# The first loads of a gated attention kernel: x's first piece in two transfers, the last two pieces merged, fifteen products of ones instead of seventeen

## The chip, the cores and the metric

The kernel runs on one core of a Trainium2 chip. Its time is the device time of one execution in microseconds (us). Several executions are timed and the median is given; one more execution is recorded by the hardware profiler, and its own time is given beside them. The core has engines that work side by side, each with its own list of instructions: TensorE (PE, whose weight loads are listed apart as PEld), VectorE (DVE), ScalarE (ACT), GpSimd (POOL) and SyncE (SP), which here only issues transfers (DMA). Engines wait for one another through semaphores.

## The reference

The input x has 2048 rows of 512 numbers. Three things are computed from it and mixed.

```
g = sigmoid((x * gate_w).sum(-1, keepdims=True))
qkv = x @ wqkv                       # 32 heads of width 16
scores = q k^T * 16**-0.5            # keys 0 to 255 places back, else -1e9
a = (softmax(scores) @ v) @ wo
b = (sigmoid(x @ w_gate) * (x @ w_up)) @ w_down      # inner width 1376
out = g * a + (1 - g) * b
```

All inputs are 32-bit floats. The change touches only the beginning of the product that gives v, x times the value weights (the last 512 columns of `wqkv`, called `wv` in the kernel).

## The kernel before, in words

Every large product is taken in three parts so that its precision holds: each 32-bit operand is split into a high part, which is a rounded copy in the format that TensorE multiplies, and a low part, the operand less its high part. Then high times high, high times low and low times high are summed in PSUM. The high part is made by a copy (mostly on ACT, in places on DVE), the low part by a subtraction on DVE, which therefore needs the high part first.

x comes transposed, as `xT`, in four chunks of 512 rows; each chunk consists of four pieces d = 0 to 3 of 128 input columns (the partitions) by 512 rows (the free dimension, called columns of a piece below). The value weights `wv` also have four pieces d of 128 by 512. Piece d of x and piece d of `wv` belong together: v for a block of 128 rows is the sum over the four d of three products each. One piece of either is 256 KB. They land in parts of one large buffer, which the profile calls `V` (`xraw` and `wvraw` in the code). High parts go to `xh` and `w` (`wvh` in the code), low parts to `xl` and `wvl`.

The program starts like this. PE multiplies ones by ones 17 times (L222, output `warm_ps`, 256 columns each), whose result nobody reads. SP issues the transfers of the pieces in the order wv0, x0, wv1, x1, wv2, x2, wv3, x3 (L230, L231), then two transfers of query and key weights (L180) and those of the next chunks of x (L206). ACT copies each piece of `wv` to its high part (L232) and, for pieces 0 and 1, the last 256 columns of x (L239); for pieces 2 and 3 it copies all of x. DVE copies the first 256 columns of x for piece 0, in two copies of 128 columns (L238), and for piece 1 in one, and makes all the low parts (L227). An engine takes its instructions in this written order.

PE then makes v of the first four blocks (L566, 48 products, output `vps`): for d = 0 and d = 1 in order high-high, high x with low weights, low x with high weights for the first two blocks and then again for the other two; for d = 2 each of the three kinds for all four blocks; for d = 3 block by block. In every product a block of x (128 by 128) is the operand that is loaded (PEld) and the weights (512 columns) stream past it. So `xh` of a block must be there before the load of its product begins. After that come the first projections (L300), and the long main part, in which attention, projections and the gated unit are interleaved by a written order on PE, ACT, DVE and SP (the scheduler is manual for these four; POOL is not touched here).

The order on SP matters too: the transfers share eight semaphores in turn, so that the ninth waits until the first has landed, and so on.

Of the kernel before, what the change touches and what calls it, by code (L numbers as in the profile page):

```python
# [14 lines left out]
P = 128  # L15
# [3 lines left out]
ND = D // P  # L19
# [4 lines left out]
CH = 512  # L24
# [46 lines left out]
def gated_mix_kernel(  # L71
# [11 lines left out]
    nc = tc.nc  # L83
# [68 lines left out]
    with ExitStack() as actx:  # L152
        apool = actx.enter_context(tc.tile_pool(name="apool", bufs=1))
        xh = apool.tile([P, ND, T], F32R, name="xh")
# [42 lines left out]
        xraw = Vf[:, NB * VROW + 16 - 2 * ND * CH:NB * VROW + 16].rearrange("p (c d t) -> p c d t", c=2, d=ND)  # L197
        wvraw = Vf[:, 0:ND * D].rearrange("p (d n) -> p d n", d=ND)
# [3 lines left out]
        wv_v = wv.rearrange("(c p) n -> p c n", p=P)  # L202
# [17 lines left out]
        def idle_mm(n):  # L220
            for _ in range(n):
                mm(warm_ps[:, 0:2 * P], ones[:, 0:P], ones[:, 0:2 * P], start=True, stop=True)  # L222

        idle_mm(17)

        def lower(lo, src, hi):
            nc.vector.tensor_tensor(lo, src, hi.bitcast(F32), op=ALU.subtract)  # L227

        for d in range(ND):
            nc.sync.dma_start(wvraw[:, d], wv_v[:, d])  # L230
            nc.sync.dma_start(xraw[:, 0, d], xT[0, d])  # L231
            nc.scalar.copy(wvh[:, d], wvraw[:, d])  # L232
            parts = ((0, 1), (1, 2), (2, 4)) if d == 0 else ((0, 2), (2, 4)) if d == 1 else ((0, 4),)
            parts = [slice(a * P, b * P) for a, b in parts]
            if d:
                lower(wvl[:, d], wvraw[:, d], wvh[:, d])
            for ts in parts[:-1]:
                nc.vector.tensor_copy(xh[:, d, ts], xraw[:, 0, d, ts])  # L238
            nc.scalar.copy(xh[:, d, parts[-1]], xraw[:, 0, d, parts[-1]])  # L239
            if d == 0:  # L240
                lower(wvl[:, d], wvraw[:, d], wvh[:, d])
            for ts in [slice(h * CH // 2, (h + 1) * CH // 2) for h in range(2)] if d < 2 else parts:
                lower(xl[:, d, ts], xraw[:, 0, d, ts], xh[:, d, ts])
# [48 lines left out]
        parts = {}  # L292
# [847 lines left out]
        for n, (c, f) in enumerate(steps):  # L1140
# [42 lines left out]
            for t in range(4):  # L1183
                ts = slice(t * P, (t + 1) * P)
# [79 lines left out]
```

## Time and profile before

| | |
|---|---|
| median of 3 runs | 706.84 us (706.81 to 707.37) |
| profiled execution | 706.25 us, of which the span from its first to its last instruction is 704.5 us |
| PE busy in the span | 700.3 us (99%) |
| DVE, ACT, POOL busy | 502.4 us, 436.0 us, 174.1 us |
| DMA | 127.40 MB, mean 181 GB/s |

In the rows of the timeline, the first number is the start in us from the span's beginning, the second how long the row lasts; a row can merge several instructions of one kind that follow each other (x2, x17). A bracket at the end of a row tells how long the engine had been idle before it, and what ended that. A row of SPq is the issue of a transfer, not the transfer itself.

### The profile page before, as it was taken

How to read it: one execution, taken by the hardware profiler on the slowest of the kernel's cores; microseconds unless marked ns; L12 is line 12 of the kernel's file. 1: busy time of each engine (PE TensorE's matmuls, PEld its weight loads, DVE VectorE, ACT ScalarE, POOL GpSimd, SP SyncE). 2: the span in 40 equal slices, each digit the busy share in tenths (PEclk: the TensorE clock that was granted, in tenths of full speed). 3: DMA queues.
4: the chain of work that ended last, by engine and by line, in shares of the span. 5: the costliest groups of instructions: out<-in, count | busy, mean ns of one | idle time of the engine just before them, and what ended most of it. 6: DMA issues, size and time to landing. Idle time of an engine off the chain costs nothing.

```text
span 704.5 us, 20403 instructions
## 1 busy us (share of the span) xinstructions
PE 700.3 (99%) x7721; PEld 613.2 (87%) x7721; DVE 502.4 (71%) x1488; ACT 436.0 (62%) x889; POOL 174.1 (25%) x254
## 2 busy tenths in 40 slices
PE   9999999999999999999999999999999999999998
PEld 7888888999888889999888888899998888888886
DVE  5368877777777776777777777786667868567481
ACT  6422777677677677767767767765685745435241
POOL 5200333233243233323324323332360000000000
PEclk9999999999999999999999999999999999999999
DMA  8466735746455364572755628564676879778521
GB/s 306 120 182 209 221 126 182 208 132 217 143 183 180 130 227 158 171 229 68 231 168 187 215 71 268 160 220 123 205 199 218 258 195 246 178 185 238 148 65 60
DMA packets 102685, 127.40 MB, mean 181 GB/s; under 512 B 45666, under 2 KB 62306, under 8 KB 102588
## 3 DMA queue, kind: packets, MB, share of 16 engines
q1 hardware_dynamic: 102444, 125.97, 58.7%
q8 instruction: 61, 1.00, 0.6%
q14 instruction: 36, 0.29, 0.1%
q10 hardware_dynamic: 144, 0.13, 0.1%
HBM read 71.80 MB, written 51.13 MB: 174 GB/s over the span
## 4 chain that ended last, share of the span: by engine, by line
PE 99%; DVE 0%; issue 0%
PE gu L300 29%; PE pj L300 12%; PE st L452 6%; PE s L390 6%; PE tp L667 6%; PE pd L101 5%; PE pd L99 5%; PE pd L100 5%; PE pv_st L488 5%; PE vh L704 4%; PE pv_s L488 3%; PE pv L488 2%; PE pa L99 2%; PE pa L100 2%; PE pa L101 2%; PE vps L566 2%
## 5 line engine op out<-in xcount | busy, mean ns | idle before, releaser
L396 DVE CUSTOM_DVE_ANT_0 junk<-s,mask 128x384 f32<-128x384 f32 (+2 forms) x512 | 272.0, 531 | 103.2 <-PE s L390 38.8
L300 PE MATMUL gu<-xh,w 64*128 64x512 f32 x1152 | 270.1, 391 | 0.0
L458 ACT ACTIVATE pbuf<-st 128x384 f32<-128x384 f32 x320 | 155.4, 495 | 53.3 <-PE st L452 24.3
L300 PE MATMUL gu<-xl,w 64*128 64x512 f32 x576 | 182.3, 389 | 0.0
L452 PE MATMUL st<-ring 64*128 64x384 f32 (+2 forms) x536 | 165.8, 322 | 0.0
L390 PE MATMUL s<-ring 64*128 64x384 f32 (+2 forms) x536 | 162.3, 321 | 0.0
L300 PEld LDWEIGHTS gu<-xh,w 64*128 64x128 f32 x1152 | 151.4, 184 | 10.0
L464 POOL TENSOR_SCALAR_AFFINE_SELECT pbuf<-pbuf 128x512 f32<-128x512 f32 x80 | 56.0, 700 | 260.6 <-ACT pbuf L458 245.2
L390 PEld LDWEIGHTS s<-ring 64*128 64x128 f32 x536 | 94.8, 184 | 11.8 <-DVE mx L396 1.2
L452 PEld LDWEIGHTS st<-ring 64*128 64x128 f32 x536 | 97.8, 184 | 7.6 <-issue 1.4
L458 ACT ACTIVATE V<-st 128x384 f32<-128x384 f32 (+2 forms) x192 | 81.9, 440 | 32.5 <-PE s L390 18.1
L300 PEld LDWEIGHTS gu<-xl,w 64*128 64x128 f32 x576 | 88.5, 184 | 2.7
L300 PE MATMUL pj<-xl,wqh 64*128 64x512 f32 (+1 forms) x228 | 79.2, 388 | 0.0
L300 PE MATMUL pj<-xh,wqh 64*128 64x512 f32 (+1 forms) x228 | 79.2, 389 | 0.0
L300 PE MATMUL pj<-xh,wql 64*128 64x512 f32 (+1 forms) x228 | 69.6, 388 | 0.0
L100 PE MATMUL pd<-ring,hb 128*128 128x512 f32 x160 | 62.3, 389 | 0.0
L101 PE MATMUL pd<-ring,hb 128*128 128x512 f32 x160 | 62.3, 389 | 0.0
L99 PE MATMUL pd<-ring,hb 128*128 128x512 f32 x160 | 62.3, 389 | 0.0
L95 ACT CAST hb<-V 128x512 fp32r<-128x512 f32 x40 | 24.9, 622 | 55.5 <-DVE V L876 47.5
L470 POOL TENSOR_SCALAR_AFFINE_SELECT pbuf<-pbuf 128x512 f32<-128x512 f32 x80 | 53.8, 673 | 0.0
L464 POOL TENSOR_SCALAR_AFFINE_SELECT V<-V 128x512 f32<-128x512 f32 x48 | 31.8, 663 | 76.4 <-ACT V L458 53.0
L627 ACT COPY sp<-gu 128x512 f32<-128x512 f32 x72 | 42.2, 586 | 9.8 <-PE gu L300 7.8
(157 smaller groups left out, 1387.2 us busy)
## 6 DMA issues: line engine op xcount, KB each, us to landing
gu_scratch<-sp SPq DMA_DIRECT2D x72, 256.0 KB
V<-gu_scratch SPq DMA_DIRECT2D x34, 512.0 KB
ring<-stack_scratch SPq DMA_DIRECT2D x56, 256.0 KB
stack_scratch<-sh SPq DMA_DIRECT2D x14, 512.0 KB
stack_scratch<-sl SPq DMA_DIRECT2D x14, 512.0 KB
ring<-stack_scratch SPq DMA_DIRECT2D x14, 512.0 KB
guraw<-in_wgu_dram SPq DMA_DIRECT2D x18, 256.0 KB
v_scratch<-V SPq DMA_DIRECT2D x4, 1088.0 KB
```

The costliest lines, as they stand in the source:

```text
L99: mm(ps, lh, rh, start=first, stop=False)
L100: mm(ps, lh, rl, start=False, stop=False)
L101: mm(ps, ll, rh, start=False, stop=last)
L300: return mm(pt, (wl if w == 2 else wh)[r, d], (xl if w == 1 else xh)[r, d, c * CH:(c + 1) * CH], start=k == 0 and not second, stop=k == 3 ...
L390: mm(pt[:, (k - k0) * P:(e - k0) * P], lhsT, blk(g, k, hh, 1, e - k), start=k == k0, stop=e == i + 1, skip_group_check=True,)
L396: nc.vector.tensor_tensor_reduce(junk[:, 0:n], pt[:, 0:n], mask[:, 3 * P - n:], scale=1.0, scalar=NEG, op0=ALU.add, op1=ALU.max, accum_out ...
L452: mm(pt[:, (q - j) * P:(e - j) * P], lhsT, blk(g, q, hh, 0, e - q), start=q == j, stop=e == last, skip_group_check=True,)
L458: exps.append(nc.scalar.activation(buf[:, s0:s0 + 2 * n, hh], pt[:, 0:n * P].rearrange("p (k t) -> p k t", t=HB), AF.Exp, scale=SCALE,))
L464: nc.gpsimd.affine_select(buf[:, s0:s0 + 2], buf[:, s0:s0 + 2], pattern=[[HB, 2], [0, HG], [1, HB]], compare_op=ALU.is_ge, fill=0.0, base= ...
L470: nc.gpsimd.affine_select(old, old, pattern=[[-HB, 2], [0, HG], [-1, HB]], compare_op=ALU.is_gt, fill=0.0, base=0, channel_multiplier=1,)
L488: mm(bank[32 * hh:32 * hh + w, o + k * HB:o + e * HB], vt[HB * half:HB * half + HB, v:v + w], p_run(g * NB + j, hh, half, k, e), start=fir ...
L667: return mm(tp[b][:, 0:TW], (xl if w == 1 else xh)[r, d, b * P:(b + 1) * P], tw[d][int(w == 2)][r, 0:TW], start=k == 0 and not second, sto ...
```

## The change

The first transfer of x is cut into two: its first 128 columns (rows of 512 bytes), then the other 384. The pieces 2 and 3 of `wv` come in one transfer of 512 KB, and then pieces 2 and 3 of x in one. The transfers are now issued in the order wv0, x0 columns 0 to 127, x0 columns 128 to 511, wv1, x1, wv2 with wv3, x2 with x3: seven instead of eight. Of piece 0 the copy of columns 128 to 255 goes from DVE to ACT. Two products of ones are left out. Everything else stands as it did, so that the lines from there on have numbers higher by four.

```
-        idle_mm(17)
+        idle_mm(15)
...
         for d in range(ND):
-            nc.sync.dma_start(wvraw[:, d], wv_v[:, d])
-            nc.sync.dma_start(xraw[:, 0, d], xT[0, d])
+            if d < 3:
+                ds = slice(d, d + 1 if d < 2 else ND)
+                nc.sync.dma_start(wvraw[:, ds], wv_v[:, ds])
+                for ts in (slice(0, P), slice(P, CH)) if d == 0 else (slice(0, CH),):
+                    nc.sync.dma_start(xraw[:, 0, ds, ts], xT[0, ds, :, ts].rearrange("d p t -> p d t"))
             nc.scalar.copy(wvh[:, d], wvraw[:, d])
             parts = ((0, 1), (1, 2), (2, 4)) if d == 0 else ((0, 2), (2, 4)) if d == 1 else ((0, 4),)
             parts = [slice(a * P, b * P) for a, b in parts]
             if d:
                 lower(wvl[:, d], wvraw[:, d], wvh[:, d])
-            for ts in parts[:-1]:
+            for ts in parts[:1] if len(parts) > 1 else []:
                 nc.vector.tensor_copy(xh[:, d, ts], xraw[:, 0, d, ts])
-            nc.scalar.copy(xh[:, d, parts[-1]], xraw[:, 0, d, parts[-1]])
+            for ts in parts[min(1, len(parts) - 1):]:
+                nc.scalar.copy(xh[:, d, ts], xraw[:, 0, d, ts])
```

On SP the list begins like this before (`in_wv_dram` and `in_xT_dram` are the two inputs, `V` the buffer):

```order
L230 DMA V<-in_wv_dram 128x512
L231 DMA V<-in_xT_dram 128x512
L230 DMA V<-in_wv_dram 128x512
L231 DMA V<-in_xT_dram 128x512
L230 DMA V<-in_wv_dram 128x512
L231 DMA V<-in_xT_dram 128x512
L230 DMA V<-in_wv_dram 128x512
L231 DMA V<-in_xT_dram 128x512
```

and like this with the change:

```order
L232 DMA V<-in_wv_dram 128x512
L234 DMA V<-in_xT_dram 128x128
L234 DMA V<-in_xT_dram 128x384
L232 DMA V<-in_wv_dram 128x512
L234 DMA V<-in_xT_dram 128x512
L232 DMA V<-in_wv_dram 128x2x512
L234 DMA V<-in_xT_dram 128x2x512
```

The second piece of the weights moves from third to fourth place, and x2 can no longer land ahead of x3, nor wv2 ahead of wv3.

On ACT, after the load of its table, the list before is, up to the first weights of a projection (`w` is the high part of `wv`):

```order
L232 CAST w_70<-V 128x512
L239 CAST xh<-V 128x256
L232 CAST w_70<-V 128x512
L239 CAST xh<-V 128x256
L232 CAST w_70<-V 128x512
L239 CAST xh<-V 128x512
L232 CAST w_70<-V 128x512
L239 CAST xh<-V 128x512
L189 CAST wqh_142<-wqraw_130 128x512
```

and with the change:

```order
L235 CAST w_70<-V 128x512
L243 CAST xh<-V 128x128
L243 CAST xh<-V 128x256
L235 CAST w_70<-V 128x512
L243 CAST xh<-V 128x256
L235 CAST w_70<-V 128x512
L243 CAST xh<-V 128x512
L235 CAST w_70<-V 128x512
L243 CAST xh<-V 128x512
L189 CAST wqh_139<-wqraw_127 128x512
```

One copy of 128 columns is added between the first weights and the last half of x0; the order of the copies of pieces 2 and 3 is unchanged.

## The prediction

> **What bounds the kernel now.** First the page: how busy the engines are, and of what the chain that ended last is made.
>
> ```profile
> span 704.5 us, 20403 instructions
> PE 700.3 (99%) x7721; PEld 613.2 (87%) x7721; DVE 502.4 (71%) x1488; ACT 436.0 (62%) x889; POOL 174.1 (25%) x254
> PE 99%; DVE 0%; issue 0%
> ```
>
> PE sets the end. A change at the start is worth as much as it moves PE's first useful products, as long as nothing later lets PE wait. So I read the chain in order of time over its first 30 us:
>
> ```profile
> 0.84 3.78 PE warm_ps L222 x17
> 4.62 11.43 PE vps L566 x48
> 16.05 8.16 PE pj L300 x36
> ```
>
> The 36 products behind take 8.16/36 = 0.227 us each. At that pace the 48 products of L566 would need 10.88 us; they take 11.43. So slow clock and waits cost this stage 0.55 us, and what stands before it is the products of ones. **This bounds the whole prize to well under 1 us**, against some 1.4 us (0.2%), which is about what a measurement of this kernel tells from no change. Next the timeline, where PE begins:
>
> ```profile
> 3.52 0.62 ACT L232 CAST w<-V 128x512 fp32r<-128x512 f32 x1 [1.44 <-DMA V<-in_wv_dram]
> 4.12 0.36 DVE L238 CAST xh<-V 128x128 fp32r<-128x128 f32 x2 [4.12 <-DMA V<-in_xT_dram]
> 4.40 0.69 DVE L227 TENSOR_TENSOR wvl<-V,w 128x512 fp32r<-128x512 f32 x1
> 4.47 0.51 PEld L566 LDWEIGHTS vps<-w,xh 128*128 128x128 f32 x2 [0.33 <-ACT w L232]
> 4.50 1.12 PE L566 MATMUL vps<-w,xh 128*128 128x512 f32 x2
> 5.06 0.56 PE L566 MATMUL vps<-w,xh 128*128 128x512 f32 x1
> 5.45 0.62 PE L566 MATMUL vps<-wvl,xh 128*128 128x512 f32 x2
> L222 PE MATMUL warm_ps<-const-bfloat16-1.0 128*128 128x256 bf16 x17 | 3.8, 414 | 0.8 <-PEq L1251 0.8
> ```
>
> Of the 3.78 us of ones, 0.41 is the length of the last record, so 16 steps take 3.37 us: 0.21 us per product of 256 columns, or 0.42 for 512, nearly twice the 0.227 of later. PE runs at half pace here. The second and third useful products start 0.39 apart (5.06, 5.45), between the two paces, so the pace changes inside the second one, by this at about 5.4 us. The ones run out at 0.84 + 17 x 0.213 = 4.47, and just then the first load starts, although weights (3.52 + 0.62 = 4.14) and the first 128 columns of x (half of 0.36 after 4.12, about 4.35) are there. **The ones end the first wait**, by about 0.1 us.
>
> **The head, part by part.** Two ones less free PE at 0.84 + 15 x 0.213 = 4.04. Then the weights are last, at 4.14, if the 128 columns land sooner than the whole piece did (4.12). A quarter of the bytes, behind the same wv0, lies between wv0's landing (3.52) and 4.12; I take 3.7, and DVE's copy ends before 4.0. The first load then starts at 4.16 instead of 4.47. Its stream begins where the second load can follow; before, the second product's start less one slow pitch (5.06 - 0.42) gives 4.64, 0.17 behind the load, so now 4.33. At the slow pace products two and three start at 4.75 and 5.17; if the pace still changes at 5.4, the third does 0.23/0.42 of its work before and ends at 5.4 + 0.45 x 0.227 = 5.50. Before, the fourth started one fast pitch after 5.45, at 5.68. The head gains **0.18 us**. The second block's columns are now copied by ACT behind the weights, after the transfer of 384 columns: with that landed by 4.2 and 0.2 us for the copy they are there at 4.45, in time for 4.75. Bounds: nothing, if the 128 columns land no sooner than 4.12; 0.3 us, if the slow pace were no cost.
>
> **Piece 1 takes the gain away.** These are the rows of its chain:
>
> ```profile
> 1.72 0.43 SPq L230 DMA_DIRECT2D V<-in_wv_dram  x1
> 2.19 0.43 SPq L231 DMA_DIRECT2D V<-in_xT_dram  x1
> 5.95 0.62 ACT L232 CAST w<-V 128x512 fp32r<-128x512 f32 x1 [1.43 <-DMA V<-in_wv_dram]
> 6.61 0.69 DVE L227 TENSOR_TENSOR wvl<-V,w 128x512 fp32r<-128x512 f32 x1 [0.85 <-ACT w L232]
> 7.21 0.29 DVE L238 CAST xh<-V 128x256 fp32r<-128x256 f32 x1
> 7.62 0.30 PEld L566 LDWEIGHTS vps<-w,xh 128*128 128x128 f32 x2 [0.15 <-issue]
> 7.72 0.62 PE L566 MATMUL vps<-w,xh 128*128 128x512 f32 x2
> 4.10:5.90 1.80, 1.80 (x7) 1.21 (x6) 1.64 (x5) 0.43 (x2) 0.00 (x0) 1.00 0.96 239
> ```
>
> wv1 lands at 5.95; ACT copies it, DVE makes its low part and only then copies x1's first 256 columns, done at 7.50. PE's load idled for them until 7.62, and the product came at 7.72: from 5.45 that is ten products in 2.27 us, 0.227 each. So PE lost nothing here, but with nothing to spare: a normal load runs 0.22 us ahead of its product (10.22 and 10.45 below), this one only 0.10. The change leaves this chain as it is. So an earlier PE waits here, and the 0.18 is lost unless wv1 lands sooner. It is issued one place later, at 2.19 instead of 1.72 (the rows' step of 0.47). That is no delay in itself: it was under way for 4.2 us, with the DMA engines 0.96 busy in the last row (4.10 to 5.90), so it waits for the engines and not for its issue. What is ahead of it are the same bytes in one more transfer. Bounds: 0.2 sooner (as much as PE could use) to 0.47 later; I take **0.0**, nearest to the row of busy engines.
>
> **Pieces 2 and 3.** Here the merged transfers decide:
>
> ```profile
> 7.87 0.62 ACT L232 CAST w<-V 128x512 fp32r<-128x512 f32 x1 [0.86 <-DMA V<-in_wv_dram]
> 8.51 0.62 ACT L239 CAST xh<-V 128x512 fp32r<-128x512 f32 x1
> 9.20 0.62 ACT L232 CAST w<-V 128x512 fp32r<-128x512 f32 x1
> 9.82 0.62 ACT L239 CAST xh<-V 128x512 fp32r<-128x512 f32 x1
> 9.86 0.33 SPq L206 DMA_DIRECT2D V<-in_xT_dram  x1
> 10.22 0.87 PEld L566 LDWEIGHTS vps<-w,xh 128*128 128x128 f32 x4
> 10.45 1.07 PE L566 MATMUL vps<-w,xh 128*128 128x512 f32 x4
> 9.50:10.00 0.50, 0.50 (x4) 0.38 (x4) 0.50 (x2) 0.50 (x2) 0.00 (x0) 1.00 1.12 410
> ```
>
> Before, x2 was copied from 8.51 and x3 from 9.82. PE wants x2's high part when piece 2 begins (load 10.22, product 10.45) and had it at 9.13, 1.1 us early. Merged, x2 counts as landed with x3. x3 had landed by 9.82 (SP's next transfer, which waits for the same semaphore, goes out at 9.86). The bytes ahead are the same, so I let the pair land at 9.82: ACT copies x2 until 10.44. From the end of such a copy to the product it took 7.72 - 7.50 = 0.22 in piece 1, so piece 2 begins at 10.66 instead of 10.45: **0.21 us lost**. Bounds: the last row shows 410 GB/s and full engines, where 256 KB take 0.64 us; if the pair is done half a piece sooner (0.32), nothing is lost, and with wv1 early some 0.2 is even kept; a whole piece later (0.64) makes it 0.85 lost. I take the middle, as the bytes are equal and one fixed end goes with each merger.
>
> [...]
>
> **What else moves, and what covers it.** Behind 10.45 ACT runs later by about 1.2 us, since x2's copy, the weights' second copy and x3's copy all stand behind 9.82: 10.44, 11.06, 11.68 instead of 10.44 for the last. The work behind it:
>
> ```profile
> 10.48 1.27 ACT L189 CAST wqh<-wqraw 128x512 fp32r<-128x512 f32 x2
> 13.16 0.39 PE L566 MATMUL vps<-w,xh 128*128 128x512 f32 x1
> 14.11 0.59 ACT L570 COPY V<-vps 128x512 f32<-128x512 f32 x1 [1.08 <-PE vps L566]
> 15.88 0.39 PE L300 MATMUL pj<-xh,wqh 128*128 128x512 f32 x1
> 10.65 0.58 POOL L267 MEMSET V<- 128x256 f32 x1 [6.96 <-DMA V<-in_xT_dram]
> 18.80 0.59 ACT L324 CAST sh<-pj 128x512 fp32r<-128x512 f32 x1 [1.61 <-PE pj L300]
> ```
>
> Piece 3 is wanted at 13.16 and there at 11.7, its low parts by 12.4. The projection weights (ACT L189) end near 13.0 instead of 11.75, wanted at 15.88. The 1.08 us that ACT idled before L570 take up most of the delay, the 1.61 before L324 the rest. POOL's memset waits for the last low part of the weights and goes from 10.65 to about 11.9; L570 needs it at 14.1. If these covers failed, each would cost at most what it is late, 0.1 to 0.2 us. The added copy on ACT (about 0.2 us) ends before wv1 lands at 5.95; the shorter DVE list brings its first subtraction 0.2 us forward. One transfer less on SP (0.43) lies beside full DMA engines.
>
> **Sum.** The waits follow each other and the last decides: 0.18 gained at the head, taken back at piece 1, and 0.21 lost at piece 2. The profiled execution, 706.25 with its span of 704.5 and 1.75 around it, would become 706.46. The runs' median is 0.59 above it; on it the same 0.21 gives **707.05 us**.
>
> **Rivals.** First, **the gain is kept**: wv1 lands 0.2 sooner and the merged x by 9.4, as less is issued. For it: the merged pairs save two ends of transfers; against it: full engines. Time 706.84 - 0.18 = 706.66, at most 706.5.
>
> Second, **the change doesn't do what it says**: the first 128 columns land with the whole piece, near 4.1. Then the first load is at about 4.37, little is gained, and the later waits decide as before: 707.05 as well, so it counts with the forecast.
>
> Third, on the other side, **the slow pace goes on**. The pace changed at 5.4, that is 4.6 us after PE began at 0.84. With two ones less PE stands idle from 4.04 to about 4.3, and longer in an execution in which wv0 lands late. If what releases the pace needs unbroken work, the count begins anew at 4.3 and ends at 8.9: 3.5 us more at half pace, in which 3.5 x (1 - 0.227/0.42) = 1.6 us of work is lost. It decides as soon as the gap is longer than the switch bears; before, it bore the 0.17 us between the last of the ones (4.47) and the first stream (4.64). Time 707.05 + 1.6 = 708.65. The granted clock (third number from the end) reads 1.00 in the row of 4.10 to 5.90 too, so it doesn't show the slow stage; the products' steps do.
>
> [...]
>
> Fourth, **the merged x lands far later**, because one late DMA engine now holds up 512 KB. For it: wv1 landed 5.95 - 4.12 = 1.83 us behind x0, where a piece takes 0.64 at the full rate, so something held it up by 1.2 us. Against it: pieces 2 and 3 followed each other in 0.6 to 0.7 us before (8.51, 9.20, 9.82). Such a hold-up in the merged x costs 1.2 us: 708.25.
>
> **Chances.** Forecast with the second rival 0.71; gain kept 0.19; slow pace 0.06; late x 0.03; something later in the program that a shift by 0.2 us sets off, with either sign, 0.01. Faster by over 0.2% would need 1.4 us where 0.55 are to be had: 0.01. Slower by over 0.2%: 0.07. Within: 0.92. The forecast's bounds are 706.6 (nothing lost) to 707.7 (0.85 lost); the runs shown differ by 0.56 among themselves, and half of that on the lower side makes 706.35. The range is 706.35 to 707.8.
>
> **What would show it.** Right: the first load of L566 at about 4.2, the product of piece 1 still near 7.7, an idle PE of about 0.2 us at piece 2's first product near 10.66, released by ACT's copy, and L300 starting near 16.1. Wrong: piece 1's product at 7.55 (wv1 sooner), piece 2's at or before 10.45 (x merged lands before 9.6), or products of 512 columns at 0.42 steps beyond 6 us.

## The result, and the profile after

| | before | after |
|---|---|---|
| median of 7 runs each | 707.10 us (706.81 to 707.68) | 711.40 us (707.94 to 712.13) |
| profiled execution | 706.25 us, span 704.5 us | 712.08 us, span 710.2 us |
| PE's first useful product | 4.50 us | 7.48 us |
| PE's first projection (L300, now L304), from the chain | 16.05 us | 20.00 us |

The changed kernel is slower: the ratio is 1.0052, with a 95% interval from 1.0041 to 1.0063. That is 3.7 us by the ratio and 4.3 by the medians, at a place where the prediction put the whole prize at well under 1 us. The page after, its busy times and chain:

```profile
span 710.2 us, 20396 instructions
PE 702.3 (99%) x7719; PEld 609.0 (86%) x7719; DVE 505.2 (71%) x1487; ACT 435.4 (61%) x890; POOL 173.8 (24%) x254
PE 98%; DVE 1%; DMA 0%; ACT 0%; issue 0%
```

PE was 99% of the chain before and is 98% now, and DVE has got 1%. Where that is, the chain in order of time over the first 30 us tells (start, length, what):

```profile
0.80 2.68 DMA V<-in_wv_dram
3.50 0.63 ACT w L235
4.16 3.22 DVE wvl L227
7.48 12.52 PE vps L570 x48
20.00 8.16 PE pj L304 x36
```

Before, the products of ones led straight into the 48 products. Now the chain goes through DVE for 3.22 us, and the 48 products take 12.52 us instead of 11.43. The timeline of the changed kernel at that place:

```profile
3.50 0.62 ACT L235 CAST w<-V 128x512 fp32r<-128x512 f32 x1 [1.43 <-DMA V<-in_wv_dram]
3.68 3.66 DVE L241 CAST xh<-V 128x128 fp32r<-128x128 f32 x1 [3.68 <-DMA V<-in_xT_dram]
3.74 3.52 POOL L282 MEMSET ring<- 128x4096 f32 x1
4.16 3.18 DVE L227 TENSOR_TENSOR wvl<-V,w 128x512 fp32r<-128x512 f32 x1
5.60 0.60 ACT L243 CAST xh<-V 128x128 fp32r<-128x128 f32 x2 [1.48 <-DMA V<-in_xT_dram]
7.45 0.50 PEld L570 LDWEIGHTS vps<-w,xh 128*128 128x128 f32 x2 [3.77 <-ACT xh L243]
7.48 1.19 PE L570 MATMUL vps<-w,xh 128*128 128x512 f32 x2 [3.51 <-DVE wvl L227]
8.47 1.05 PE L570 MATMUL vps<-wvl,xh 128*128 128x512 f32 x2
10.76 0.62 PE L570 MATMUL vps<-wvl,xh 128*128 128x512 f32 x2
10.80 0.62 ACT L243 CAST xh<-V 128x512 fp32r<-128x512 f32 x1 [1.43 <-DMA V<-in_xT_dram]
14.40 1.07 PE L570 MATMUL vps<-w,xh 128*128 128x512 f32 x4
```

The first 128 columns of x0 do land early, at 3.68, as they should. But their copy on DVE, which took about 0.2 us before, takes 3.66. Beside it stands an instruction that was not there before: POOL zeroes the first ring buffer from 3.74 to 7.26, and DVE's copy and the subtraction behind it end with it. Before, this zeroing ran from 11.07 on. The page and the diff don't show why, but the lists of POOL do. Before (from L258 on, in the kernel's line numbers):

```
L258 AFFINE_SELECT mask<-mask 128x128
L264 MEMSET fr 1x1024
L267 MEMSET V 128x256
L278 MEMSET ring 128x4x1024 x3
L267 MEMSET V 128x256
```

and after:

```
L262 AFFINE_SELECT mask<-mask 128x128
L268 MEMSET fr 1x1024
L282 MEMSET ring 128x4x1024
L271 MEMSET V 128x256
L282 MEMSET ring 128x4x1024 x2
L271 MEMSET V 128x256
```

POOL is the one engine whose order isn't written out by hand; a scheduler chooses it. With the change it put the zeroing of the first ring buffer ahead of V's memset, which waits for the low weights. So the zeroing, which waits for nothing, starts as soon as POOL is free.

The second part of the loss is the pace. Busy times and granted clock (third number from the end) in three windows of the changed kernel:

```profile
3.60:7.00 3.40, 0.37 (x3) 0.08 (x1) 3.32 (x2) 1.83 (x5) 3.34 (x2) 1.00 0.91 318
7.00:10.40 3.40, 2.92 (x7) 2.37 (x8) 3.26 (x9) 0.94 (x2) 0.26 (x1) 0.50 0.98 341
10.40:13.80 3.40, 3.40 (x16) 2.79 (x16) 2.34 (x4) 3.00 (x6) 0.99 (x2) 1.00 1.05 403
```

PE was nearly idle in the first window at full clock (0.37 us busy, clock 1.00), worked in the second at half clock (2.92 us, 0.50), and had the full clock again in the third (1.00). (The column reads 1.00 until the trace's first clock record, which is at 3.59 here and at 5.39 in the kernel before; so it doesn't show the half pace of the ones, and the 5.39 bears out the 5.4 that the prediction read from the products' steps.) The two products at 8.47 take 1.05 us for what takes 0.62 at 10.76. By the profiles, the first product is 7.48 - 4.50 = 2.98 us late, and until the first projection another 0.97 is added, mostly by the slow pace: 20.00 - 16.05 = **3.95 us of the 4.3**. An estimate from the paces agrees: at half pace a product takes 0.425 us (two from 8.47 to 9.32), later 0.23 (two from 10.76 to 11.22), so from 7.48 to 10.4 PE loses 2.9 x (1 - 0.23/0.425) = 1.3 us, where the kernel before lost some 0.35 until 5.4.

### The profile page after: what moved, and what is told of

Its sections match the earlier page's. It is cut to its first block, busy times and chain, and to the rows that moved or that the text cites. A ratio compares the mean times of both kernels' runs of the same rounds, so it can differ in the third digit from the quotient of the medians.

```text
span 710.2 us, 20396 instructions
## 1 busy us (share of the span) xinstructions
PE 702.3 (99%) x7719; PEld 609.0 (86%) x7719; DVE 505.2 (71%) x1487; ACT 435.4 (61%) x890; POOL 173.8 (24%) x254
## 4 chain that ended last, share of the span: by engine, by line
PE 98%; DVE 1%; DMA 0%; ACT 0%; issue 0%
PE gu L304 29%; PE pj L304 12%; PE st L456 7%; PE tp L671 6%; PE s L394 6%; PE pd L100 5%; PE pd L101 5%; PE pd L99 5%; PE pv_st L492 5%; PE vh L708 4%; PE pv_s L492 3%; PE pv L492 2%; PE pa L99 2%; PE pa L100 2%; PE pa L101 2%; PE vps L570 2%
## 5 line engine op out<-in xcount | busy, mean ns | idle before, releaser
L304 PE MATMUL gu<-xh,w 64*128 64x512 f32 x1152 | 269.7, 391 | 0.0
L304 PE MATMUL gu<-xl,w 64*128 64x512 f32 x576 | 182.2, 389 | 0.0
L304 PEld LDWEIGHTS gu<-xh,w 64*128 64x128 f32 x1152 | 150.6, 184 | 11.8
L304 PEld LDWEIGHTS gu<-xl,w 64*128 64x128 f32 x576 | 88.2, 184 | 3.2
L304 PE MATMUL pj<-xl,wqh 64*128 64x512 f32 (+1 forms) x228 | 79.1, 389 | 0.0
L304 PE MATMUL pj<-xh,wqh 64*128 64x512 f32 (+1 forms) x228 | 79.1, 389 | 0.0
L304 PE MATMUL pj<-xh,wql 64*128 64x512 f32 (+1 forms) x228 | 69.5, 388 | 0.0
```

The source lines that it names most:

```text
L304: return mm(pt, (wl if w == 2 else wh)[r, d], (xl if w == 1 else xh)[r, d, c * CH:(c + 1) * CH], start=k == 0 and not second, stop=k == 3 ...
```

## The experiments

Two theories stood against each other: that POOL's new order did it, or that the divided and merged transfers, or the ones, did it by themselves. The first four kernels ran side by side (kernel before there: 707.43 us, 17 runs).

**POOL's order mended.** The changed kernel with the zeroings tied behind V's memset:

```
-        fill_v(0, NB // 2)
+        v_ones = fill_v(0, NB // 2)
...
-            nc.gpsimd.memset(ring[r].bitcast(F32), 0.0)
+            after(nc.gpsimd.memset(ring[r].bitcast(F32), 0.0), v_ones)
```

> The changed kernel, with the three zeroings of the ring on POOL tied behind the memset of ones into V, as they stood before the change; loads, copies and fifteen products of ones as changed. Theory POOL: the loss comes from the first zeroing of the ring, which the change put ahead of V's memset and which held DVE's first copy from 3.7 to 7.3; without it the copy takes 0.2 us, the first load of L570 starts at 4.2, the first product of piece 2 near 10.7, and the time is 706.5 to 707.6 (the prediction's own sum was 707.05). Theory LOADS: the divided and merged transfers or the two ones less do it by themselves; then the first useful product stays near 7.5 and the time near 711.

Measured: 709.85 us, ratio 1.0030 (1.0018 to 1.0042). Neither theory's time came. From its timeline:

```profile
3.61 0.23 DVE L241 CAST xh<-V 128x128 fp32r<-128x128 f32 x1 [3.61 <-DMA V<-in_xT_dram]
4.10 0.69 PE L570 MATMUL vps<-w,xh 128*128 128x512 f32 x1
6.07 0.61 ACT L243 CAST xh<-V 128x128 fp32r<-128x128 f32 x2 [2.02 <-DMA V<-in_xT_dram]
6.42 0.50 PE L570 MATMUL vps<-w,xh 128*128 128x512 f32 x1 [1.63 <-ACT xh L243]
```

The copy is back at 0.23 us and the first product comes at 4.10, even earlier than I expected. But the second comes at 6.42: x0's other 384 columns landed near 6.07, not by 4.2. So there is a second loss, which POOL's stall had covered.

**The zeroing first, in the kernel before.** Only POOL's order is changed:

```
-        fill_v(0, NB // 2)
+        ring_0 = nc.gpsimd.memset(ring[0].bitcast(F32), 0.0)
+        v_ones = fill_v(0, NB // 2)
+        after(v_ones, ring_0)
...
-        for r in range(RING):
-            nc.gpsimd.memset(ring[r].bitcast(F32), 0.0)
+        for r in range(1, RING):
+            after(nc.gpsimd.memset(ring[r].bitcast(F32), 0.0), v_ones)
```

> The kernel before, with the zeroing of the first ring buffer tied ahead of V's memset on POOL, and nothing else moved: loads, seventeen ones and copies as before. Theory POOL: DVE's copies of x0, which start at 4.12 before, end near 7.3, the first useful product comes near 7.4 and the time is 710 to 712.5. Theory LOADS: POOL's order is of no matter, 706.8 to 707.5.

Measured: 711.60 us, ratio 1.0060 (1.0047 to 1.0073), with seventeen ones and every load as before:

```profile
3.74 3.52 POOL L269 MEMSET ring<- 128x4096 f32 x1
4.20 3.20 DVE L238 CAST xh<-V 128x128 fp32r<-128x128 f32 x2 [4.20 <-DMA V<-in_xT_dram]
7.48 0.98 PE L568 MATMUL vps<-w,xh 128*128 128x512 f32 x2 [2.95 <-DVE xh L238]
```

POOL's order by itself makes a loss as large as the whole change.

**The mergers alone,** in the kernel before:

```
-            nc.sync.dma_start(wvraw[:, d], wv_v[:, d])
-            nc.sync.dma_start(xraw[:, 0, d], xT[0, d])
+            if d < 3:
+                ds = slice(d, d + 1 if d < 2 else ND)
+                nc.sync.dma_start(wvraw[:, ds], wv_v[:, ds])
+                nc.sync.dma_start(xraw[:, 0, ds], xT[0, ds].rearrange("d p t -> p d t"))
```

> The kernel before with only the last two pieces of x and of the value weights merged; x0 in one transfer, seventeen ones. In its list on POOL the first zeroing of the ring stands ahead of V's memset, as in the changed kernel. Theory POOL: 710 to 712.5, first useful product near 7.4. Theory LOADS with the divided x0 or the fifteen ones to blame: 707.0 to 707.4 (the 0.2 us of the prediction's piece 2).

Measured: 711.45 us, ratio 1.0059 (1.0044 to 1.0074).

```profile
3.74 3.52 POOL L280 MEMSET ring<- 128x4096 f32 x1
4.30 3.11 DVE L240 CAST xh<-V 128x128 fp32r<-128x128 f32 x2 [4.30 <-DMA V<-in_xT_dram]
7.49 0.80 PE L568 MATMUL vps<-w,xh 128*128 128x512 f32 x2 [2.86 <-DVE xh L240]
```

So it is the merger that makes the scheduler turn POOL's list (why, and whether the merged weights or the merged x do it, these kernels don't show); none of the kernels here that keep pieces 2 and 3 apart has the zeroing first, but for the one in which it was put there.

**The change without the mergers,** POOL's list as before:

```
-            if d < 3:
-                ds = slice(d, d + 1 if d < 2 else ND)
-                nc.sync.dma_start(wvraw[:, ds], wv_v[:, ds])
-                for ts in (slice(0, P), slice(P, CH)) if d == 0 else (slice(0, CH),):
-                    nc.sync.dma_start(xraw[:, 0, ds, ts], xT[0, ds, :, ts].rearrange("d p t -> p d t"))
+            nc.sync.dma_start(wvraw[:, d], wv_v[:, d])
+            for ts in (slice(0, P), slice(P, CH)) if d == 0 else (slice(0, CH),):
+                nc.sync.dma_start(xraw[:, 0, d, ts], xT[0, d, :, ts])
```

> The changed kernel without the mergers: x0 in two transfers, second block's copy on ACT, fifteen ones, but pieces 2 and 3 in transfers of their own. In its list on POOL V's memset stands first, as before the change. Theory POOL: 706.5 to 707.1, first load near 4.2, with the product of piece 1 near 7.7 as before. Theory LOADS: near 711 with the slow pace beyond 6 us.

Measured: 709.45 us (707.02 to 711.66 in 12 runs), ratio 1.0026 (1.0013 to 1.0038).

```profile
3.67 0.23 DVE L239 CAST xh<-V 128x128 fp32r<-128x128 f32 x1 [3.67 <-DMA V<-in_xT_dram]
4.16 0.80 PE L568 MATMUL vps<-w,xh 128*128 128x512 f32 x1
5.78 0.61 ACT L241 CAST xh<-V 128x128 fp32r<-128x128 f32 x2 [1.68 <-DMA V<-in_xT_dram]
6.13 0.50 PE L568 MATMUL vps<-w,xh 128*128 128x512 f32 x1 [1.18 <-ACT xh L241]
```

Again neither theory's time came. The divided x0 costs some 2 us of its own. Its 384 columns land at 5.8, about where wv1 landed before (5.95); both were third on the queue. The next four kernels test that and three other points (kernel before beside them: 706.90 us, 29 runs).

**A whole x0 in third place.** The kernel before with wv1 issued ahead of x0:

```
-            nc.sync.dma_start(wvraw[:, d], wv_v[:, d])
-            nc.sync.dma_start(xraw[:, 0, d], xT[0, d])
+            for k, (dst, src) in enumerate(((wvraw, wv_v), (xraw[:, 0], xT[0]))):
+                for e in ((0, 1), ()) [d] if k == 0 and d < 2 else (d,):
+                    nc.sync.dma_start(dst[:, e], src[:, e] if k == 0 else src[e])
```

> The kernel before with one transfer moved: wv1 is issued ahead of x0, so that x0, whole, in rows of 2 KB, is the third on the queue; ones, copies and POOL's list as before. Theory PLACE: whatever is third lands at 5.6 to 6.1, as wv1 did before (5.95) and x0's 384 columns do with the change (5.60, 5.78, 6.07 in three profiles); the first useful product then comes near 6.2 and the time is 1.3 to 2.2 us above the kernel before. Theory PIECE: x0's 384 columns were late because they are cut out of x0 (rows of 1.5 KB, a second pass over the same piece); a whole x0 in third place then lands one piece later than in second, near 4.8, and the time is 0.3 to 0.8 us above the kernel before.

Measured: 709.59 us, ratio 1.0033 (1.0024 to 1.0042), a little above the upper end for the place.

```profile
5.85 0.40 ACT L240 CAST xh<-V 128x256 fp32r<-128x256 f32 x1 [1.78 <-DMA V<-in_xT_dram]
6.22 0.70 PE L567 MATMUL vps<-w,xh 128*128 128x512 f32 x2 [1.59 <-DVE xh L239]
```

Uncut, in rows of 2 KB, x0 lands at 5.85 in third place, where it landed at 4.12 in second. So it is the place and not the cut. The traces record the landing of a transfer in sixteen parts, and only some parts of the third are late: eleven of x0's are there by 5.08 here, the last five at 5.56 to 5.83; in the changed kernel fourteen of the third transfer's are there by 4.75, the last two at 5.54 and 5.58, and the two transfers behind it have two late parts each as well. In all these kernels the third transfer is under way at about the same time (issued at 1.72 us in the kernel before, landed at 5.06 to 6.52 in all), so the runs don't tell its place from that time.

**All of x0 copied by ACT,** POOL's list as changed:

```
-            for ts in parts[:1] if len(parts) > 1 else []:
+            for ts in parts[:1] if d == 1 else []:
                 nc.vector.tensor_copy(xh[:, d, ts], xraw[:, 0, d, ts])
-            for ts in parts[min(1, len(parts) - 1):]:
+            for ts in parts[1 if d == 1 else 0:]:
                 nc.scalar.copy(xh[:, d, ts], xraw[:, 0, d, ts])
```

> The changed kernel with its list on POOL as it is (the first zeroing of the ring ahead), but the first 128 columns of x0 copied by ACT, not DVE, so that DVE's first work is the subtraction for the low weights. Theory COPY: the zeroing holds only a copy on DVE; the subtraction runs 4.2 to 4.9 beside it, the first load starts near 4.4, and what is left is the late 384 columns: 709 to 710.3, as with POOL's order mended. Theory ENGINE: it holds whatever DVE begins; the low weights are done near 7.3, and the time is 710.7 to 712.

Measured: 709.17 us, ratio 1.0030 (1.0018 to 1.0042).

```profile
3.74 3.53 POOL L282 MEMSET ring<- 128x4096 f32 x1
4.11 0.69 DVE L227 TENSOR_TENSOR wvl<-V,w 128x512 fp32r<-128x512 f32 x1 [4.11 <-ACT w L235]
4.33 0.50 PE L570 MATMUL vps<-w,xh 128*128 128x512 f32 x1
5.06 0.61 ACT L243 CAST xh<-V 128x128 fp32r<-128x128 f32 x2 [0.79 <-DMA V<-in_xT_dram]
5.41 0.50 PE L570 MATMUL vps<-w,xh 128*128 128x512 f32 x1 [0.58 <-ACT xh L243]
```

Beside the same zeroing the subtraction takes its usual 0.69 us. So the zeroing held DVE's copies, not DVE; in the changed kernel the subtraction only stood behind the copy. The four profiles with the zeroing first agree: in three, the copies last 3.66 us (one) and 3.20 and 3.11 (two each), and in this one the subtraction runs through in 0.69. Why a copy is held and the subtraction isn't, no run shows.

**The mergers with POOL's order mended** (the two edits shown above together, in the kernel before):

> The kernel before with the last two pieces of x and of the value weights merged, and the ring's zeroings tied behind V's memset on POOL as before; x0 whole and second, seventeen ones. Theory of the prediction (piece 2 waits for the merged x): 0.21 us above the kernel before (bounds 0 to 0.85), piece 2's first product near 10.7, released by ACT. If the merged x is as late as in the profile of the kernel with POOL's order mended (copied from 10.93): piece 2's first product near 11.8 and 1.3 us above the kernel before.

Measured: 707.04 us, ratio 1.0003 (0.9995 to 1.0012).

```profile
5.47 1.05 PE L568 MATMUL vps<-wvl,xh 128*128 128x512 f32 x2
6.52 0.62 ACT L234 CAST w<-V 128x512 fp32r<-128x512 f32 x1 [2.01 <-DMA V<-in_wv_dram]
9.72 0.62 ACT L241 CAST xh<-V 128x512 fp32r<-128x512 f32 x1 [0.62 <-DMA V<-in_xT_dram]
10.92 0.87 PEld L568 LDWEIGHTS vps<-w,xh 128*128 128x128 f32 x4
11.15 1.07 PE L568 MATMUL vps<-w,xh 128*128 128x512 f32 x4
```

Without POOL's turn the mergers cost nothing that can be measured. The merged x lands by 9.72 and its copy ends at 10.34; in this execution PE wants it at 10.92, since it was itself later, and doesn't wait. The 0.21 us of the prediction lies within the interval, so it is neither shown nor excluded.

**Fifteen ones alone** (`idle_mm(17)` to `idle_mm(15)` in the kernel before):

> The kernel before with fifteen products of ones instead of seventeen, and nothing else. Theory POOL and PLACE: no measurable change, within 0.4 us of the kernel before, pace changing by 5.4 as before. The prediction's third rival (the slow pace goes on because of the gap): 1.2 to 1.7 us above it, products at 0.42 steps beyond 6 us.

Measured: 707.23 us, ratio 1.0003 (0.9994 to 1.0011). No change, as expected; the pace changed near 6.1 here, not by 5.4 as expected (two products take 0.73 us from 5.53 to 6.26, between 0.45 at full and 0.85 at half pace; the clock record is at 6.11):

```profile
4.53 1.19 PE L566 MATMUL vps<-w,xh 128*128 128x512 f32 x2 [0.34 <-DVE xh L238]
5.53 0.90 PE L566 MATMUL vps<-wvl,xh 128*128 128x512 f32 x2
6.26 0.63 PE L566 MATMUL vps<-w,xl 128*128 128x512 f32 x2
```

The last two ran beside a kernel before of 707.25 us (23 runs). **The 384 columns on ACT's queue,** in the kernel without the mergers:

```
-                nc.sync.dma_start(xraw[:, 0, d, ts], xT[0, d, :, ts])
+                (nc.scalar if ts.start else nc.sync).dma_start(xraw[:, 0, d, ts], xT[0, d, :, ts])
```

> The changed kernel without the mergers (as no_merge), but x0's 384 columns issued by ACT at the very start, beside SP's first transfers, so that wv1 is again third on SP's queue. If the place on SP's queue makes a transfer late: the 384 columns land by 4.2, PE's first product comes near 4.2 to 4.3 and the second by 4.8, the time is within 0.5 us of the kernel before, possibly 0.2 below it. If it is the third transfer of all, on whichever queue, or the cut itself: the second product again near 6 and the time 1.5 to 2.5 us above it.

Measured: 708.50 us (706.99 to 710.41 in 12 runs), ratio 1.0018 (1.0008 to 1.0028). Neither expectation held:

```profile
4.74 0.62 ACT L233 CAST w<-V 128x512 fp32r<-128x512 f32 x1 [2.22 <-DMA V<-in_wv_dram]
5.12 0.23 DVE L239 CAST xh<-V 128x128 fp32r<-128x128 f32 x1 [5.12 <-DMA V<-in_xT_dram]
5.49 0.71 PE L568 MATMUL vps<-w,xh 128*128 128x512 f32 x2 [1.29 <-ACT w L233]
```

With two queues at once wv0 itself lands at 4.74 instead of 3.5, and the first product comes at 5.49. In this profile the other queue only moves the delay to the front.

**The kernel before, again,** for a second profile:

> The kernel before, unchanged, for a second profile of it. The first profiled execution was the fastest of all of its runs; in a usual one PE should be 0.3 to 1.0 us later by the end without being later at piece 1, and the moment at which the pace changes should differ from 5.4.

Measured: 707.11 us, ratio 0.9997 (0.9987 to 1.0006); its profiled execution took 707.61, with a span of 705.7.

```profile
4.51 1.19 PE L566 MATMUL vps<-w,xh 128*128 128x512 f32 x2
5.07 0.62 ACT L232 CAST w<-V 128x512 fp32r<-128x512 f32 x1 [0.52 <-DMA V<-in_wv_dram]
```

It starts like the first, but its pace changes later (clock record at 5.85 instead of 5.39). It is 0.23 us behind the first by the first projection (16.28 instead of 16.05), and 1.2 by the end; level at piece 1, and 0.3 to 1.0 by the end, was expected. So part of the 5.7 us between the first two profiles' spans (710.2 and 704.5) is the luck of the first one. Against this second span it is 4.5.

## Why the prediction was wrong

It forecast 707.05 us, 706.35 to 707.8, and gave slower by over 0.2% a chance of 0.07. The time was 711.40.

**The step that failed first** is a sentence of "What else moves": POOL's memset of V goes from 10.65 to about 11.9. The zeroing of the ring behind it isn't mentioned, so it was put at nothing, as if it followed as before. I followed the change through the lists of SP and ACT and took POOL's to be untouched, because the diff has no line of POOL; "everything else stands as it did", in the section on the change, holds for the code and not for POOL's list. There the zeroing went ahead, from 11.07 to 3.74, and DVE's copy took 3.66 us. The first expected term, 0.18 us gained at the head, became 2.98 lost. The zeroing by itself is enough for the whole loss (711.60 and 711.45 in the two kernels that have it with x0 whole).

**The second failing step** is in the head: "with that landed by 4.2", said of the 384 columns. I reasoned by bytes: what is ahead of them is the same as before. In second place, x0 had landed by 4.12, so the rest of it should have, too. Yet the row of wv1 (third, landed 1.83 us behind x0) stood in the prediction. I read it as a hold-up by "one late DMA engine" and feared it for the merged x alone. No run shows that the late ones of the sixteen parts are DMA engines, and it is the third transfer in which they come first (five with x0 in third place, two in the changed kernel): x0's columns took that place, and landed 0.9 to 2.0 us later than x0 had before (5.06 to 6.07 in the four profiles in which they are third). In the result this loss is hidden: they land at 5.60, while DVE holds PE until 7.48. Alone it costs about 2 us (ratio 1.0026, 1.0030, 1.0030 and 1.0033, or 1.8 to 2.3 us, and 2.0 to 2.7 by the medians, in the four kernels in which x0 or its rest is third and no copy on DVE is held). The losses do not add, because PE waits for the later of the two.

**Piece 1 and piece 2**, the terms on which the sum rested, were not put to the test: both pieces had landed long before PE came. Piece 2's first product came at 14.40, with x2 copied by 11.42. With POOL mended the mergers lie between 0.4 us gained and 0.8 lost (interval 0.9995 to 1.0012), which holds the 0.21.

**The rivals.** "The gain is kept" didn't happen in any kernel. "The first 128 columns land with the whole piece" is refuted: with all transfers on SP's queue they land at 3.6 to 3.7. "The merged x lands far later" came true in part: it landed at 10.80 in the changed kernel and at 10.93 with POOL's order mended, some 1 us behind the 9.82 that I took, but at 9.72 with the mergers alone and POOL mended; PE was itself so late that it didn't wait for it. "The slow pace goes on" was right that the slow pace can follow idle time of PE, and wrong about which: after the gap that two ones less leave it cost nothing that can be measured (1.0003), but it came after the 3.51 us in which PE waited for DVE, and cost about 0.97 us there, where I had 1.6. The three profiles with a held copy all have a stage of 3.4 us at half clock at this place (here from 7.01 to 10.42; mean granted clock of the execution 0.998), the nine others have none (0.999 to 1.000). PE's wait for DVE is 2.86 to 3.51 us in the three; the longest waits at this place among the nine are 1.63 us (POOL's order mended) and 1.59 (x0 third). How long a wait must be for the slow pace, these runs don't show.

**What held:** two ones less cost and bring nothing that can be measured (the copy moved to ACT was not tried alone); the first load comes at 4.1 to 4.2 once DVE is free; the delay of ACT behind 10.45 let PE wait nowhere in the changed kernel, which came late itself. No kernel gained, so the bound of 0.55 us on the prize was not put to the test. What made the range too narrow is that the head was given bounds from nothing to 0.3 us gained, and no loss at all; the losses in the range were piece 2's.

Some 0.4 us of the 4.3 are not placed. The first two profiles differ by another 1.75 us after the first projection (5.7 less 3.95), but the kernel before differs from itself by 1.2 with almost the same start, so this can't be read off single executions. The price of the slow pace is such a reading too: with the mergers alone, two of four executions show a full granted clock (711.52 and 711.72) and were no faster than the two others (711.18 and 711.38). None of the kernels tried is faster than the kernel before.

## What to carry to other kernels

Compare the lists of every engine, above all those whose order a scheduler chooses: a change in the transfers of one engine can move work on another that the diff doesn't name. A bound on what can be won is no bound on what can be lost. At the start of these kernels the whole x0 landed at 4.12 us in second place on the queue and at 5.85 in third, 1.73 later with one piece of 256 KB more ahead of it, so the x0 that is wanted first should not have been divided over the second and the third place.

## What the runs showed of the hardware that I had not expected

- A zeroing on POOL of 128 by 4096 floats (3.52 us) held a copy on DVE of 128 by 128 until it ended (3.66 instead of 0.23 us), but not a subtraction (0.69 either way). In the changed kernel the copy's record begins at 3.68, ahead of the zeroing's at 3.74, and is held all the same. The one execution that was much faster than the others (707.94) also had the highest granted clock of the seven (0.999, the others 0.996 to 0.998). It would fit a copy that came through first; that wasn't seen in a profile.
- The third transfer of the program landed at 5.1 to 6.5 us in every profile with one queue, wv1 and x0 alike (5.95, 5.07, 6.52; 5.60, 6.07, 5.78, 5.06, 5.85), the second, where it was a whole piece, at 4.1 to 4.3. It is some of its sixteen parts that are late (five at 5.56 to 5.83 with x0 in third place, two at 5.54 and 5.58 in the changed kernel). What holds them back was not found; with a second queue at the same time wv0 landed at 4.74 instead of 3.5 us.
- PE's pace changed at a moment that differs from one execution to the next: at 5.39 in the first profile, at 6.11 with fifteen ones, and at 6.81 with POOL's order mended for the mergers (by the clock records; there the two products at 5.47 still take 1.05 us), without a measurable difference between these kernels' medians.
